# Decode attention with a gated FFN: FFN weights and FFN moved into the K/V loop, projections cut into four column tiles

## The chip, the cores and the metric

The kernel runs on one core of a Trainium2 chip. The metric is device time in microseconds (us) of one execution. A timed execution is a little longer than the span that the profile shows for it (118.14 us for a span of 116.4). The profile is one execution taken by the hardware profiler; "the granted clock" is the share of full speed that the chip gave to the matrix engine (PE). The other engines are DVE (vector), ACT (scalar), POOL and SP; SP issues most of the DMA.

## The reference, cut to what matters

Two rows of 448 numbers go through one decode step. About three quarters of the bytes loaded (32 transfers of 1 MB, out of 44 MB) are the K and V caches of the last 2048 positions.

```python
xn = _layernorm(x)                                  # x: [2, 1, 448]
q = (xn @ wq)                                       # 16 heads of 256, 8 K/V heads
p = softmax(q k^T * 256**-0.5)                      # last W = 2048 of 8192 positions
s = (p v) @ wo                                      # wo: [4096, 448]
g = silu(relu(xn @ w1) @ w2)                        # w1: [448, 1792], w2: [1792, 448]
return x + s * g
```

## The kernel before

One queue (SP) loads everything but the small x, in one order: K0, K1, wq, K2 to K5, V0, V1, then K and V in turn, each transfer 1 MB, and behind the last V the FFN weights w1 and w2 (1.6 MB each) and then wo in five pieces (3.7 MB). wo uses the buffer of wq. Every engine works through its own list in program order.

The loop has eight steps for each K/V head pair k. Work of different pairs is interleaved by step: transpositions of K (`do_T`) run ahead, scores and softmax follow, and the products with V (`do_PV`) come two pairs later:

```python
for k in range(NPAIR):
    e = NCH * k                                     # NCH = 8, NPAIR = 8
    at_step(max(e + 5, NCH - 1), 2, lambda k=k: do_S(k, 0))
    at_step(e + 9, 2, lambda k=k: do_S(k, 1))
    # ... the softmax chain of the pair in steps e + 9 to e + 14
    for s in range(0, NCH, 2):
        at_step(e + 2 * NCH + s, 3, lambda k=k, s=s: do_PV(k, s))
        at_step(e + 2 * NCH + s, 3, lambda k=k, s=s: do_PV(k, s + 1))
```

So step 32 has the transposition of K8 and then the first product with V4. The second argument of `at_step` is the order within a step.

Behind the loop stand the FFN, the gate and the output projection; both products are a single row of full-width matmuls:

```python
for f in range(14):                                 # second FFN product
    m_f = pr.op(PE, mm(sbk[0][0:2, 0:D], h_sb[:, 2 * f:2 * f + 2], w2_sb[:, f * D:(f + 1) * D],
                       f == 0, f == 13), deps)
# ... gate on [2, 448]: exp, + 1, reciprocal, times
for j in range(32):                                 # output projection, D = 448
    m_o = pr.op(PE, mm(obk[0][0:B, 0:D], at2[:, 2 * j:2 * j + 2], wqo[:, j * D:(j + 1) * D],
                       j == 0, j == 31), deps)
# ... times g, plus x, one store of [2, 448]
```

## Time and profile before

| what | value |
|---|---|
| median of three runs | 119.11 us (119.05 to 119.46) |
| span of the profiled execution | 116.4 us (that execution took 118.14 us) |
| DMA stream | about 418 GB/s from 14 us until 107 us |
| last K/V tile landed | 92.9 us |
| last piece of wo landed | 109.3 us |
| attention done (last operand of the projection ready) | 99.3 us |

The landing times are read from the trace's semaphore records. A tile counts as landed when the last of its 16 parts has.

Three rows of the page of the kernel before, in 40 equal slices of the span; a digit is a share in tenths:

```profile
PE   0039828777989498868988977898898365969990
PEclk9999976999999999967999996799999975599999
DMA  3998999999999999999999999999999999999200
```

The DMA is at nine tenths until the 37th slice. The PE is busy throughout, and its clock falls in four places. Next, the timeline of the PE of the kernel before. Columns are start, duration, engine, line of the kernel, operation, output<-inputs, sizes, count, and in brackets the idle time before it and what ended that. L240 is the line of a helper through which most matmuls go, so look at the tile names.

```profile
40.58 0.39 PE L240 MATMUL obk<-vbuf,pt 128*4 128x256 bf16 x8 [1.14 <-DMA vbuf<-in_A_v_cache_dram]
50.56 0.59 PE L240 MATMUL obk<-vbuf,pt 128*4 128x256 bf16 x8 [1.15 <-DMA vbuf<-in_A_v_cache_dram]
60.66 0.39 PE L240 MATMUL obk<-vbuf,pt 128*4 128x256 bf16 x8
70.51 0.39 PE L240 MATMUL obk<-vbuf,pt 128*4 128x256 bf16 x8 [1.01 <-DMA vbuf<-in_A_v_cache_dram]
...
88.89 0.39 PE L240 MATMUL obk<-vbuf,pt 128*4 128x256 bf16 x8
...
98.93 4.10 PE L240 MATMUL sbk<-w_sb,xr 128*4 128x448 bf16 x14
104.64 2.81 PE L240 MATMUL sbk<-w_sb,h_sb 128*2 128x448 bf16 x14 [0.37 <-DVE h_sb L454]
107.28 6.22 PE L240 MATMUL obk<-wqo,at 128*2 128x448 bf16 x32
```

The first product with V of a pair starts at 40.58, 50.56, 60.66 and 70.51 us. Three of the four waited about 1 us for their V tile: the DMA sets the pace. From 88.89 us on there are only the products of the last two pairs and the last pair's chain, and from 98.93 the FFN and the projection in series. The end of the kernel before, all engines without weight loads:

```profile
108.46 2.94 DVE L464 RECIPROCAL tmp<-ea 2x448 f32<-2x448 f32 x1
113.53 0.61 DVE L475 TENSOR_TENSOR tmp<-obk,g_sb 2x448 f32<-2x448 f32 x1 [1.49 <-PE obk L240]
114.18 0.61 DVE L477 TENSOR_TENSOR out_sb<-tmp,x_sb 2x448 bf16<-2x448 f32 x1
114.82 0.31 SPq L36 DMA_DIRECT2D out_dram<-out_sb  x1
```

The reciprocal of the gate (2.94 us on only two partitions) is hidden by the projection. Two further vector operations and the store follow it.

### The profile page before, as it was taken

What the parts mean: (1) busy time and instruction counts of PE and PEld (TensorE: products, weight loads), DVE (VectorE), ACT (ScalarE), POOL (GpSimd) and SP (SyncE); (2) the same over time, 40 slices, a digit from 0 to 9 for tenths busy, and PEclk for the clock granted to TensorE, in tenths of its full rate; (3) what the DMA queues carried; (4) which work ended last, traced back from release to release, by engine and by line L of the source; (5) the groups of instructions that cost most, each with busy time, mean ns of one, the idle gap of its engine ahead of it and who ended that gap; (6) DMA issues with size and microseconds to landing.
All of it is one profiled execution on the core that took longest, in us unless ns stands there. A gap on an engine that the chain in (4) does not pass through costs nothing.

```text
span 116.4 us, 2511 instructions
## 1 busy us (share of the span) xinstructions
PE 86.2 (74%) x1108; PEld 52.7 (45%) x1108; DVE 54.5 (47%) x122; ACT 45.3 (39%) x57; POOL 1.5 (1%) x10
## 2 busy tenths in 40 slices
PE   0039828777989498868988977898898365969990
PEld 0039701445666355634655653566564142334430
DVE  2085401473565654626377371737636443140854
ACT  5913810069565338403834832273673200000100
POOL 5000000000000000000000000000000000000000
PEclk9999976999999999967999996799999975599999
DMA  3998999999999999999999999999999999999200
GB/s 68 420 500 384 453 386 428 417 411 425 425 406 422 425 408 420 425 408 425 417 406 428 414 411 428 417 408 428 422 403 428 435 405 416 436 399 373 85 0 1
DMA packets 5907, 44.27 MB, mean 380 GB/s; under 512 B 645, under 2 KB 905, under 8 KB 1289
## 3 DMA queue, kind: packets, MB, share of 16 engines
q1 hardware_dynamic: 5892, 44.11, 91.6%
q8 instruction: 9, 0.15, 0.5%
q14 instruction: 2, 0.01, 0.0%
q10 hardware_dynamic: 4, 0.00, 0.0%
HBM read 44.11 MB, written 0.00 MB: 379 GB/s over the span
## 4 chain that ended last, share of the span: by engine, by line
DMA 41%; PE 37%; DVE 12%; ACT 5%; issue 1%; SPq 1%; ACTq 0%
DMA vbuf<-in_A_v_cache_dram 41%; PE tb L261 13%; PE obk L240 10%; PE sbk L240 10%; PE mbk L240 4%; DVE o_sb L343 2%; DVE mrow L298 2%; DVE kt L269 2%; DVE rm L290 2%; PE mbk L316 1%; ACT L217 1%; ACT L211 1%; DVE xg L220 1%; ACT obk L211 1%; ACT sbk L211 1%
## 5 line engine op out<-in xcount | busy, mean ns | idle before, releaser
L271 ACT ACTIVATE kt<-tb 128x1024 bf16<-128x1024 bf16 x32 | 32.6, 1024 | 44.0 <-PE tb L261 44.0
L261 PE MATMUL tb<-ident,kbuf 128*128 128x128 bf16 x512 | 41.5, 233 | 0.0
L261 PEld LDWEIGHTS tb<-ident,kbuf 128*128 128x128 bf16 x512 | 33.8, 106 | 7.3 <-issue 7.1
L269 DVE COPY kt<-tb 128x1024 bf16<-128x1024 bf16 x32 | 22.1, 690 | 10.4 <-PE tb L261 10.4
L240 PE MATMUL obk<-vbuf,pt 128*4 128x256 bf16 x256 | 13.4, 297 | 3.5 <-DMA vbuf<-in_A_v_cache_dram 3.5
L240 PE MATMUL sbk<-kt,qz 128*4 128x512 bf16 x128 | 10.8, 407 | 0.6 <-DVE qz L381 0.6
L290 DVE TENSOR_REDUCE rm<-sbk 128x1 f32<-128x512 f32 x8 | 5.5, 692 | 11.1 <-PE sbk L240 11.1
L240 PEld LDWEIGHTS obk<-vbuf,pt 128*4 128x4 bf16 x256 | 4.0, 85 | 7.2 <-DMA vbuf<-in_A_v_cache_dram 4.2
L309 ACT ACTIVATE e_sb<-sbk,bias 128x512 bf16<-128x512 f32 x8 | 5.5, 687 | 3.1 <-DVE bias L305 3.1
L343 DVE TENSOR_SCALAR o_sb<-obk,rs 128x512 bf16<-128x512 f32 x8 | 5.9, 734 | 1.6 <-PE obk L240 1.6
L240 PE MATMUL obk<-wqo,at 128*2 128x448 bf16 x32 | 6.2, 352 | 0.0
L461 ACT ACTIVATE ea<-sbk 2x448 f32<-2x448 f32 x1 | 0.5, 533 | 14.3 <-PE sbk L240 14.3
L240 PE MATMUL mbk<-ident,xg 2*128 2x2 bf16 x7 | 0.3, 164 | 7.7 <-DVE xg L220 7.7
L240 PE MATMUL mbk<-one_f,mrow 1*128 1x1 f32 x16 | 3.0, 256 | 3.8 <-DVE mrow L298 3.8
L321 DVE COPY pt<-mbk 128x64 bf16<-128x64 bf16 x8 | 1.5, 192 | 9.1 <-PE mbk L316 9.1
L298 DVE TENSOR_REDUCE mrow<-mbk 1x128 f32<-1x512 f32 x8 | 5.4, 671 | 0.4 <-PE mbk L295 0.4
L240 PE MATMUL mbk<-fold,o_sb 128*128 128x2 bf16 x32 | 2.0, 168 | 4.4 <-DVE o_sb L343 4.4
L240 PE MATMUL obk<-wqo,xr 128*4 128x512 bf16 x28 | 3.1, 620 | 2.7 <-DMA wqo<-in_A_wq_dram 2.7
L240 PEld LDWEIGHTS mbk<-one_f,mrow 1*128 1x128 f32 x16 | 2.3, 182 | 5.2 <-DVE mrow L298 5.2
L316 PE MATMUL mbk<-ident,e_sb 128*128 128x128 bf16 x32 | 3.2, 222 | 1.6 <-ACT e_sb L309 1.6
L240 PEld LDWEIGHTS obk<-wqo,at 128*2 128x2 bf16 x32 | 2.7, 84 | 3.4
L240 PE MATMUL sbk<-w_sb,xr 128*4 128x448 bf16 x14 | 4.1, 465 | 0.0
(59 smaller groups left out, 47.4 us busy)
## 6 DMA issues: line engine op xcount, KB each, us to landing
kbuf<-in_A_k_cache_dram SPq DMA_DIRECT2D x16, 1024.0 KB, 20.2
vbuf<-in_A_v_cache_dram SPq DMA_DIRECT2D x16, 1024.0 KB, 24.2
wqo<-in_A_wq_dram SPq DMA_DIRECT2D x1, 3584.0 KB, 15.0
w_sb<-in_B_w_dram SPq DMA_DIRECT2D x2, 1568.0 KB, 28.8
wqo<-in_A_wo_dram SPq DMA_DIRECT2D x2, 1120.0 KB, 28.5
wqo<-in_A_wo_dram SPq DMA_DIRECT2D x1, 896.0 KB, 27.7
wqo<-in_A_wo_dram SPq DMA_DIRECT2D x2, 224.0 KB, 25.3
x_sb<-in_A_x_dram ACTq DMA_DIRECT2D x1, 1.8 KB
```

What stands on the lines that cost most here:

```text
L211: a_z = [pr.op(ACTE, lambda e, t=t: e.memzero(t[:, :])) for t in (obk[0], sbk[0], sbk[1], obk[1])]
L217: a_sd = pr.op(ACTE, lambda e: e.activation(sd[0:B, 1:2], sd[0:B, 0:1], ACT.Sqrt), [v_ve])
L240: return lambda e: e.matmul(out_ap, lhsT=lhsT, rhs=rhs, start=start, stop=stop, skip_group_check=True, **kw)
L261: o = pr.op(PE, lambda e, n=n, lo=lo: e.matmul(bank[:, n * 128:(n + 1) * 128], lhsT=src[:, lo:lo + 128], rhs=ident[:, :], start=True, stop ...
L269: evac[i] = pr.op(DVE, lambda e: e.tensor_copy(dst[:, :], bank[:, :]), deps)
L271: evac[i] = pr.op(ACTE, lambda e: e.activation(dst[:, :], bank[:, :], ACT.Copy), deps)
L290: st["rm", k] = pr.op(DVE, lambda e: e.tensor_reduce(out=rm[k % 2][:, :], in_=sbk[k % 2][:, :], axis=AX.X, op=ALU.max), [st["S", k], st.ge ...
L298: st["mrow", k] = pr.op(DVE, lambda e: e.tensor_reduce(out=view(mrow[k % 2], 0, [[32, 4], [1, 32]], n=1), in_=view(mbk, 0, [[0, 4], [1, 32 ...
L309: st["exp", k] = pr.op(ACTE, lambda e: e.activation(e_sb[k % 2][:, :], sbk[k % 2][:, :], ACT.Exp, bias=bias[k % 2][:, 0:1], accum_out=ssum ...
L316: o = pr.op(PE, lambda e, j=j: e.matmul(mb16[:, 512 + 128 * j:640 + 128 * j], lhsT=e_sb[k % 2][:, 128 * j:128 * j + 128], rhs=ident[:, :], ...
L321: st["pt", k] = pr.op(DVE, lambda e: e.tensor_copy(view(pt[k % NP], 0, [[16, 4], [4, 4], [1, 4]]), view(mb16, 512, [[128, 4], [32, 4], [1, ...
L343: st["osb", k] = pr.op(DVE, lambda e: e.tensor_scalar(out=o_sb[k % 2][:, :], in0=obk[k % 2][:, :], scalar1=rs[:, k:k + 1], scalar2=None, o ...
```

## The change

Its intent is to empty the tail. The FFN weights are loaded in the middle of the K/V stream, and the FFN runs inside the loop. The second FFN product and the output projection are cut into four column tiles of 112 columns that go to four separate 32-column strips of the PE, so that four matmuls run at once, and gate and last operations work on 112 columns instead of 448 (on all 128 partitions, eight of which hold results), and the store takes those eight. One score bank is given up for a bank of the FFN.

```diff
+        x_c = named("x_c", [128, NCOL], BF)          # NCOL = D // 4 = 112
+        d_xc = [pr.dma(ACTE, view(x_c, 0, [[1, NCOL]], n=4, p0=b, pstep=32), ...) for b in range(B)]
-        sbk = [psum(f"sbk{i}", [128, 512], F32) for i in range(2)]
+        sbk = psum("sbk", [128, 512], F32)
+        fbk = psum("fbk", [128, 512], F32)
+        for n, fn in enumerate((lambda: do_H(0), lambda: do_H(1), do_hT, do_F)):
+            at_step(4 * NCH + 1 + 2 * n, 6, fn)
         for k in range(NPAIR):
+            if k == 2:
+                loads += [(load_w1, 0, 1), (load_w2, 0, 1)]
             ...                                     # K 2k+4, K 2k+5, V 2k, V 2k+1
-        d_w1 = pr.dma(SP, w1_sb[:, :], w1_src)       # behind the loop
-        d_w2 = pr.dma(SP, w2_sb[:, :]..., w2_src)
         ...
-            m_f = pr.op(PE, mm(sbk[0][0:2, 0:D], h_sb[...], w2_sb[:, f * D:(f + 1) * D], ...
+                for i in range(4):
+                    lo = f * D + i * NCOL
+                    o = pr.op(PE, mm(fbk[32 * i:32 * i + B, 0:NCOL], h_sb[...], w2_sb[:, lo:lo + NCOL],
+                                     f == 0, f == 13, tile_position=(0, 32 * i)), deps)
         ...                                         # the projection in the same way, 32 x 4
-        d_o = pr.dma(SP, out[:, 0, :], out_sb[0:B, :], [v_o])
+        d_o = [pr.dma((SP, ACTE)[b], out[b, 0, :].rearrange("(i n) -> i n", i=4), ...) for b in range(B)]
```

More of the change, by code (lines that the diff above doesn't have):

```diff
@@ L109, in bass_recurrent_scan__sliding_block_cached__dense_activation_relu__decode_kernel @@
     WO_PARTS = [10, 10, 8, 2, 2]
+    NCOL = D // 4
     es = contextlib.ExitStack()
@@ L119, in psum, with view @@
             return es.enter_context(nc.psum_tensor(name, shape, dt))
-        def view(t, off, dims, n=128, p0=0):
+        def view(t, off, dims, n=128, p0=0, pstep=1):
             width = t.shape[1]
-            return bass.AP(t, p0 * width + off, [[width, n]] + dims)
+            return bass.AP(t, p0 * width + off, [[width * pstep, n]] + dims)
         ident = named("ident", [128, 128], BF)
@@ L143, in bass_recurrent_scan__sliding_block_cached__dense_activation_relu__decode_kernel @@
         h_sb = named("h_sb", [128, 28], BF)
-        ea = named("ea", [128, D], F32)
-        g_sb = named("g_sb", [128, D], F32)
-        tmp = named("tmp", [128, D], F32)
-        out_sb = named("out_sb", [128, D], BF)
+        x_c = named("x_c", [128, NCOL], BF)
+        ea = named("ea", [128, NCOL], F32)
+        g_sb = named("g_sb", [128, NCOL], F32)
+        tmp = named("tmp", [128, NCOL], F32)
+        out_sb = named("out_sb", [128, NCOL], BF)
         rm = [named(f"rm{i}", [128, 1], F32) for i in range(2)]
@@ L179, in bass_recurrent_scan__sliding_block_cached__dense_activation_relu__decode_kernel @@
         d_x = pr.dma(ACTE, x_sb[0:B, :], A_x[:, 0, :])
+        p_xc = pr.op(POOL, lambda e: e.memset(x_c[:, :], 0.0))
+        d_xc = [pr.dma(ACTE, view(x_c, 0, [[1, NCOL]], n=4, p0=b, pstep=32),
+                       A_x[b, 0, :].rearrange("(i n) -> i n", i=4), [p_xc]) for b in range(B)]
         d_k, d_v = {}, {}
@@ L209, in bass_recurrent_scan__sliding_block_cached__dense_activation_relu__decode_kernel @@
         p_qz = pr.op(POOL, lambda e: e.memset(qz[:, :], 0.0), [p_one])
-        a_z = [pr.op(ACTE, lambda e, t=t: e.memzero(t[:, :])) for t in (obk[0], sbk[0], sbk[1], obk[1])]
+        a_z = [pr.op(ACTE, lambda e, t=t: e.memzero(t[:, :])) for t in (obk[0], sbk, obk[1], fbk)]
         v_bn = pr.op(DVE, lambda e: e.bn_stats(st6[0:B, :], x_sb[0:B, :]), [d_x])
@@ L273, in do_S @@
         def do_S(k, b):
-            bank = sbk[k % 2]
-            deps = [st["q"], a_z[2]] + ([st.get(("exp", k - 2))] if b == 0 else [])
+            bank = sbk
+            deps = [st["q"], a_z[1]] + ([st.get(("exp", k - 1))] if b == 0 else [])
             for dhi in range(2):
@@ L290, in ch_max @@
             st["rm", k] = pr.op(DVE, lambda e: e.tensor_reduce(
-                out=rm[k % 2][:, :], in_=sbk[k % 2][:, :], axis=AX.X, op=ALU.max),
+                out=rm[k % 2][:, :], in_=sbk[:, :], axis=AX.X, op=ALU.max),
                 [st["S", k], st.get(("rmT", k - 2))])
@@ L309, in ch_exp @@
             st["exp", k] = pr.op(ACTE, lambda e: e.activation(
-                e_sb[k % 2][:, :], sbk[k % 2][:, :], ACT.Exp, bias=bias[k % 2][:, 0:1],
+                e_sb[k % 2][:, :], sbk[:, :], ACT.Exp, bias=bias[k % 2][:, 0:1],
                 accum_out=ssum[k % 2][:, 0:1]), [st["bsb", k], st.get(("Pt", k - 2)), st.get(("gs", k - 2))])
@@ L333, in do_PV @@
             bank, src, p = obk[k % 2], vbuf[c % NVB], pt[k % NP]
-            deps = [d_v[c], st["pt", k], a_z[3]] + ([st.get(("osb", k - 2)), st["q"]] if s == 0 else [])
+            deps = [d_v[c], st["pt", k], a_z[2]] + ([st.get(("osb", k - 2)), st["q"]] if s == 0 else [])
             for i in range(4):
@@ L383, in do_q, with do_H, do_hT, do_F @@
                         view(mb16, 256 * r + b, [[2, 2], [32, 4], [128, 2]])), [o, p_qz])
+        def do_H(u):
+            deps = [st["w1"], a_z[3], st.get("h_n")]
+            for s in range(SLOTS):
+                lo = s * FC + u * (FC // 2)
+                o = pr.op(PE, mm(fbk[0:4, 0:FC // 2], xr[:, 4 * s:4 * s + 4], w1_sb[:, lo:lo + FC // 2],
+                                 s == 0, s == SLOTS - 1), deps)
+                deps = []
+            st["h_n"] = pr.op(DVE, lambda e: e.tensor_scalar(
+                out=h_n[0:4, u * (FC // 2):(u + 1) * (FC // 2)], in0=fbk[0:4, 0:FC // 2],
+                scalar1=0.0, scalar2=None, op0=ALU.max), [o])
+        def do_hT():
+            deps = [st["h_n"]]
+            for j in range(7):
+                o = pr.op(PE, mm(fbk[:, 4 * j:4 * j + 4], view(h_n, j, [[7, 128]], n=4), ident[0:4, 0:4], j == 0), deps)
+                deps = []
+            st["hT"] = pr.op(DVE, lambda e: e.tensor_copy(
+                view(h_sb, 0, [[2, 7], [14, 2], [1, 2]]), view(fbk, 0, [[4, 7], [2, 2], [1, 2]])), [o])
+        def do_F():
+            deps = [st["w2"], st["hT"]]
+            for f in range(14):
+                for i in range(4):
+                    lo = f * D + i * NCOL
+                    o = pr.op(PE, mm(fbk[32 * i:32 * i + B, 0:NCOL], h_sb[:, 2 * f:2 * f + 2], w2_sb[:, lo:lo + NCOL],
+                                     f == 0, f == 13, tile_position=(0, 32 * i)), deps)
+                    deps = []
+            a_e = pr.op(ACTE, lambda e: e.activation(ea[:, :], fbk[:, 0:NCOL], ACT.Exp, scale=-1.0), [o])
+            v_d = pr.op(DVE, lambda e: e.tensor_scalar(
+                out=ea[:, :], in0=ea[:, :], scalar1=1.0, scalar2=None, op0=ALU.add), [a_e])
+            v_rc = pr.op(DVE, lambda e: e.reciprocal(tmp[:, :], ea[:, :]), [v_d])
+            st["g"] = pr.op(DVE, lambda e: e.tensor_tensor(
+                out=g_sb[:, :], in0=fbk[:, 0:NCOL], in1=tmp[:, :], op=ALU.mult), [v_rc])
+        def load_w1(_):
+            st["w1"] = pr.dma(SP, w1_sb[:, :], w1_src)
+        def load_w2(_):
+            st["w2"] = pr.dma(SP, w2_sb[:, :].rearrange("p (hf f) -> p hf f", hf=2), w2_src)
         steps = {}
@@ L424, in bass_recurrent_scan__sliding_block_cached__dense_activation_relu__decode_kernel @@
         assert not loads
-        d_w1 = pr.dma(SP, w1_sb[:, :], w1_src)
-        d_w2 = pr.dma(SP, w2_sb[:, :].rearrange("p (hf f) -> p hf f", hf=2), w2_src)
         d_wo = []
@@ L438, in bass_recurrent_scan__sliding_block_cached__dense_activation_relu__decode_kernel @@
             view(at2, 0, [[2, 32], [1, 2]]), view(mbk, 256, [[1, 32], [32, 2]])), [m_at])
-        deps = [d_w1, st["exp", NPAIR - 2], st["exp", NPAIR - 1]]
-        for u in range(2):
-            for s in range(SLOTS):
-                lo = s * FC + u * (FC // 2)
-                m_h = pr.op(PE, mm(sbk[u][0:4, 0:FC // 2], xr[:, 4 * s:4 * s + 4], w1_sb[:, lo:lo + FC // 2],
-                                   s == 0, s == SLOTS - 1), deps)
-                deps = []
-            v_h = pr.op(DVE, lambda e, u=u: e.tensor_scalar(
-                out=h_n[0:4, u * (FC // 2):(u + 1) * (FC // 2)], in0=sbk[u][0:4, 0:FC // 2],
-                scalar1=0.0, scalar2=None, op0=ALU.max), [m_h])
-        deps = [v_h, v_at2]
-        for j in range(7):
-            m_t = pr.op(PE, mm(mbk_ap(4 * j, 4), view(h_n, j, [[7, 128]], n=4), ident[0:4, 0:4], j == 0), deps)
-            deps = []
-        v_ht = pr.op(DVE, lambda e: e.tensor_copy(
-            view(h_sb, 0, [[2, 7], [14, 2], [1, 2]]), view(mbk, 0, [[4, 7], [2, 2], [1, 2]])), [m_t])
-        deps = [d_w2, v_ht]
-        for f in range(14):
-            m_f = pr.op(PE, mm(sbk[0][0:2, 0:D], h_sb[:, 2 * f:2 * f + 2], w2_sb[:, f * D:(f + 1) * D],
-                               f == 0, f == 13), deps)
-            deps = []
-        a_e = pr.op(ACTE, lambda e: e.activation(ea[0:B, :], sbk[0][0:B, 0:D], ACT.Exp, scale=-1.0), [m_f])
-        v_d = pr.op(DVE, lambda e: e.tensor_scalar(
-            out=ea[0:B, :], in0=ea[0:B, :], scalar1=1.0, scalar2=None, op0=ALU.add), [a_e])
-        v_rc = pr.op(DVE, lambda e: e.reciprocal(tmp[0:B, :], ea[0:B, :]), [v_d])
-        v_g = pr.op(DVE, lambda e: e.tensor_tensor(
-            out=g_sb[0:B, :], in0=sbk[0][0:B, 0:D], in1=tmp[0:B, :], op=ALU.mult), [v_rc])
-        deps = [v_at2, st["osb", NPAIR - 2]]
+        deps = [v_at2, st["g"]]
         landed = dict(d_wo)
@@ L471, in bass_recurrent_scan__sliding_block_cached__dense_activation_relu__decode_kernel @@
             deps = deps + [landed.get(j)]
-            m_o = pr.op(PE, mm(obk[0][0:B, 0:D], at2[:, 2 * j:2 * j + 2], wqo[:, j * D:(j + 1) * D],
-                               j == 0, j == 31), deps)
-            deps = []
+            for i in range(4):
+                lo = j * D + i * NCOL
+                m_o = pr.op(PE, mm(fbk[32 * i:32 * i + B, 0:NCOL], at2[:, 2 * j:2 * j + 2], wqo[:, lo:lo + NCOL],
+                                   j == 0, j == 31, tile_position=(0, 32 * i)), deps)
+                deps = []
         v_t = pr.op(DVE, lambda e: e.tensor_tensor(
-            out=tmp[0:B, :], in0=obk[0][0:B, 0:D], in1=g_sb[0:B, :], op=ALU.mult), [m_o, v_g])
+            out=tmp[:, :], in0=fbk[:, 0:NCOL], in1=g_sb[:, :], op=ALU.mult), [m_o, st["g"]])
         v_o = pr.op(DVE, lambda e: e.tensor_tensor(
-            out=out_sb[0:B, :], in0=tmp[0:B, :], in1=x_sb[0:B, :], op=ALU.add), [v_t])
-        d_o = pr.dma(SP, out[:, 0, :], out_sb[0:B, :], [v_o])
-        pr.op(SP, None, [d_o])
+            out=out_sb[:, :], in0=tmp[:, :], in1=x_c[:, :], op=ALU.add), [v_t, *d_xc])
+        d_o = [pr.dma((SP, ACTE)[b], out[b, 0, :].rearrange("(i n) -> i n", i=4),
+                      view(out_sb, 0, [[1, NCOL]], n=4, p0=b, pstep=32), [v_o]) for b in range(B)]
+        pr.op(SP, None, d_o)
         with nc.Block() as block:
```

## The prediction

> **What bounds it now.** To 70.5 us, the DMA stream: the slices show DMA at 9 of 10 until 107 us, about 418 GB/s, and in the timeline the PE comes early to the first PV of each pair and waits for V, released at 40.58, 50.56 and 70.51 us after 1.0 to 1.2 us idle. A K/V pair lands per 10.0 us; the PE needs 8.8 us for eight steps (60.66 to 69.5). From 70.5 to 88.9 the PE paces, then pair 7's softmax chain (to 99.3), then, in the chain of waits, a serial tail: first FFN product 4.05, relu and transposes 1.6, second product 2.81 (to 107.44), output projection 6.07 (32 matmuls of 448 columns), two DVE ops 1.23, store 1.57. The reciprocal (2.94) hides under the projection. The last weights land near 109.3, so bytes alone would allow a gain of 4 us.
>
> **What the change does.**
> 1. Tail: 8.4 us of FFN leave it. The projection becomes 128 matmuls of 112 columns. Four-tile PV matmuls of 256 columns take 40 ns each (0.32 per 8), more than a quarter of their 107 ns of columns: something per instruction limits them. The Trainium skill, "TensorEngine Tiling (Array Packing)", Instruction Overhead, gives each matmul about 60 cycles however few its columns. Estimate: 128 x 40 to 48 ns = 5.1 to 6.1 us, at most 1 saved. Last DVE ops: 0.26 each, 0.7 saved.
> 2. Loop: w1 and w2 (3.8 us each) stand ahead of K8, K9, V4, V5. K8 lands at 53.6 instead of 46.0, V4 at 58.1 instead of 50.5. The PE works in program order; the PV that needs V4 is in step 32, the FFN in steps 33 to 39, behind it. So the PE, there at 49.4, idles some 8 us (one transposition between) where it idled 1.15, and only then does the FFN: it doesn't fill the hole that its own weights made.
> 3. After the hole: from 58.2, PE work of 8.8 + 8.8 + 8.8 + 8.3, FFN 5.6 (14 x 0.19, transposes 0.35, 56 x 45 ns), and 1.4 for half clock. The skill, "TensorE: Matmul & The Clock Gate", Part 1, says an idle window of 3.4 us halves the clock until a busy one; the trace has 0.5-clock stretches of 3.41 us, the one at 50.4 cost 1.4. Sum: 99.9 at the point that was 88.9. V6 to V15 then land ahead of use (V15 at 100.5); only the 1.0 wait and the dip at 70.5 vanish (counted).
> 4. Pair 7's chain 10.4: 110.3. Projection 5.7: 116.0. DVE 0.55, store 1.6: span 118.1, against 116.4.
>
> The single score bank costs nothing: exp ends 0.35 us before the next scores start. The extra small loads delay the start about 1 us, hidden behind wq (16.7).
>
> **Prediction.** 119.11 + 1.75 = 120.9 us, 118.3 to 123.3. Faster by over 2%: 0.06; within 2%: 0.60; slower by over 2%: 0.34.
>
> **What would show it.** Right: two PE gaps of about 4 us between 49 and 58, ended by K and V loads, granted clock 0.5 after; no later V wait; the eight steps with FFN 15 to 16.5 us; attention done at 109 to 112; projection 5 to 6.3; DMA idle before it ends. Wrong: PE idle there under 4 us, or attention done before 107.
>
> **What would make it wrong.** Tiled matmuls at 25 ns (4 us less in all); the FFN filling waits; a half clock lasting longer; a DMA stall as K14 waits for freed buffers.

## The result and the profile after

The changed kernel takes 117.89 us (117.46 to 118.09, four runs) against 119.10 us of the kernel before in the same rounds. The ratio is 0.9887, with a 95% interval of 0.985 to 0.9923: 1.1% faster. Ratios in this document are the mean time of one kernel's fast runs over that of the other's fast runs of the same rounds, so they are not quite the ratio of the medians that are quoted. Executions over 1.5% slower than the fastest of the same kernel are left out of the means.

The PE's row and its clock on the page of the changed kernel:

```profile
PE   0009945967989689503099898988988988567480
PEclk9999999997699999985559999999999999965569
```

There is now a hole in the PE's row from the 17th to the 20th slice, and the clock is at half for three slices there. The DMA's row has hardly changed (not shown). The timeline of the PE of the changed kernel, in the places shown of before (L246 is the helper now, L267 the transpositions):

```profile
52.90 1.03 PE L267 MATMUL tb<-ident,kbuf 128*128 128x128 bf16 x8 [4.25 <-DMA kbuf<-in_A_k_cache_dram]
57.87 0.60 PE L246 MATMUL obk<-vbuf,pt 128*4 128x256 bf16 x8 [3.94 <-DMA vbuf<-in_A_v_cache_dram]
60.17 2.17 PE L246 MATMUL fbk<-w_sb,xr 128*4 128x448 bf16 x7
64.56 1.49 PE L246 MATMUL fbk<-w_sb,xr 128*4 128x448 bf16 x7
68.27 0.53 PE L246 MATMUL fbk<-ident,h_n 4*128 4x4 bf16 x7
71.08 0.86 PE L246 MATMUL fbk<-w_sb,h_sb 128*2 128x112 bf16 x56
72.42 0.39 PE L246 MATMUL obk<-vbuf,pt 128*4 128x256 bf16 x8
...
98.51 0.39 PE L246 MATMUL obk<-vbuf,pt 128*4 128x256 bf16 x8
...
109.51 2.97 PE L246 MATMUL fbk<-wqo,at 128*2 128x112 bf16 x119 [0.32 <-DVE at L485]
112.95 0.31 PE L246 MATMUL fbk<-wqo,at 128*2 128x112 bf16 x9 [0.47 <-issue]
```

The PE waits 4.25 us for K8 and 3.94 us for V4, and only then, from 60.17 us, come the four FFN groups. The point that was 88.89 us (first product with V of the pair 6) is 98.51 us. The projection begins at 109.51 instead of 107.28, but it is over at 113.3 instead of 113.5 us. Inside it, before the last nine matmuls, stands an idle time of 0.47 us ended by "issue", that is by nothing that the profile shows. The end:

```profile
113.29 0.28 DVE L497 TENSOR_TENSOR tmp<-fbk,g_sb 128x112 f32<-128x112 f32 x1 [3.84 <-PE fbk L246]
113.60 0.28 DVE L499 TENSOR_TENSOR out_sb<-tmp,x_c 128x112 bf16<-128x112 f32 x1
113.91 0.64 SPq L36 DMA_DIRECT2D out_dram<-out_sb  x1
113.91 0.56 ACTq L36 DMA_DIRECT2D out_dram<-out_sb  x1
```

The two last vector operations take 0.28 us each instead of 0.61. The store is slower: from the end of the last vector operation to the landing it takes 1.99 us (113.88 to 115.87) instead of 1.18 (114.79 to 115.97).

Piece by piece, predicted and measured (us):

| piece | predicted | measured | read from |
|---|---|---|---|
| PE idle before V4 | about 8 | 8.2 | brackets at 52.90 and 57.87 |
| eight steps with the FFN | 15.8 | 14.55 | 57.87 to 72.42 |
| of it second FFN product | 2.5 | 0.8 | 71.08 to the next start, 71.87 |
| next 24 steps | 25.9 | 26.1 | 72.42 to 98.51 |
| last pair's chain | 10.4 | 11.0 | 98.51 to 109.51 |
| projection | 5.7 | 3.8 | 109.51 to 113.27 |
| last vector operations | 0.55 | 0.6 | 113.29 to 113.88 |
| store and end | 1.6 | 2.4 | 113.88 to 116.3 |
| span | 118.1 | 116.3 | |

The chain is longer by 0.6 us; it ran at half clock from 102.5 us on, and its four small transpositions, for one, took 0.61 us instead of 0.40. The large differences are the two tiled products: together 3.6 us less than predicted.

### The profile page after: what moved, and what is told of

It is laid out like the page before. It is cut to its first block, busy times and chain, and to the rows that moved or that the text cites. A ratio compares the mean times of both kernels' runs of the same rounds, so it can differ in the third digit from the quotient of the medians.

```text
span 116.3 us, 2783 instructions
## 1 busy us (share of the span) xinstructions
PE 80.1 (69%) x1246; PEld 53.3 (46%) x1246; DVE 50.8 (44%) x122; ACT 45.1 (39%) x57; POOL 1.6 (1%) x11
## 4 chain that ended last, share of the span: by engine, by line
DMA 36%; PE 36%; DVE 18%; ACT 4%; issue 2%; SPq 1%
DMA vbuf<-in_A_v_cache_dram 23%; DMA wqo<-in_A_wq_dram 13%; PE tb L267 11%; PE fbk L246 7%; PE obk L246 6%; PE sbk L246 6%; DVE kt L275 5%; PE mbk L246 4%; DVE o_sb L349 3%; DVE rm L296 3%; DVE mrow L304 3%; PE mbk L322 2%; ACT e_sb L315 1%; ACT L315 1%; SPq L36 1%
## 5 line engine op out<-in xcount | busy, mean ns | idle before, releaser
L267 PE MATMUL tb<-ident,kbuf 128*128 128x128 bf16 x512 | 41.9, 235 | 4.2 <-DMA kbuf<-in_A_k_cache_dram 4.2
L267 PEld LDWEIGHTS tb<-ident,kbuf 128*128 128x128 bf16 x512 | 34.2, 107 | 11.2 <-issue 6.6
L246 PE MATMUL obk<-vbuf,pt 128*4 128x256 bf16 x256 | 13.4, 297 | 4.5 <-DMA vbuf<-in_A_v_cache_dram 4.5
L246 PE MATMUL sbk<-kt,qz 128*4 128x512 bf16 x128 | 10.3, 392 | 1.9 <-ACT e_sb L315 1.4
L296 DVE TENSOR_REDUCE rm<-sbk 128x1 f32<-128x512 f32 x8 | 5.5, 691 | 10.4 <-PE sbk L246 10.4
L246 PEld LDWEIGHTS obk<-vbuf,pt 128*4 128x4 bf16 x256 | 4.0, 85 | 8.2 <-DMA vbuf<-in_A_v_cache_dram 4.9
L246 PE MATMUL mbk<-ident,xg 2*128 2x2 bf16 x7 | 0.3, 163 | 8.9 <-DVE xg L226 8.9
L246 PE MATMUL mbk<-one_f,mrow 1*128 1x1 f32 x16 | 3.0, 256 | 3.9 <-DVE mrow L304 3.9
L246 PE MATMUL mbk<-fold,o_sb 128*128 128x2 bf16 x32 | 2.0, 167 | 4.4 <-DVE o_sb L349 4.4
L246 PEld LDWEIGHTS mbk<-one_f,mrow 1*128 1x128 f32 x16 | 2.3, 182 | 5.4 <-DVE mrow L304 5.4
L246 PEld LDWEIGHTS mbk<-ident,xg 2*128 2x128 bf16 x7 | 0.3, 101 | 8.9 <-DVE xg L226 8.9
L246 PEld LDWEIGHTS mbk<-fold,o_sb 128*128 128x128 bf16 x32 | 1.4, 99 | 6.0 <-DVE o_sb L349 6.0
L322 PEld LDWEIGHTS mbk<-ident,e_sb 128*128 128x128 bf16 x32 | 2.0, 106 | 4.0 <-issue 3.0
L246 PE MATMUL fbk<-wqo,at 128*2 128x112 bf16 x128 | 3.3, 292 | 0.8 <-issue 0.5
L246 PE MATMUL fbk<-w_sb,xr 128*4 128x448 bf16 x14 | 3.7, 409 | 0.0
```

The lines of the kernel that those rows point to most:

```text
L246: return lambda e: e.matmul(out_ap, lhsT=lhsT, rhs=rhs, start=start, stop=stop, skip_group_check=True, **kw)
L267: o = pr.op(PE, lambda e, n=n, lo=lo: e.matmul(bank[:, n * 128:(n + 1) * 128], lhsT=src[:, lo:lo + 128], rhs=ident[:, :], start=True, stop ...
L296: st["rm", k] = pr.op(DVE, lambda e: e.tensor_reduce(out=rm[k % 2][:, :], in_=sbk[:, :], axis=AX.X, op=ALU.max), [st["S", k], st.get(("rmT ...
L322: o = pr.op(PE, lambda e, j=j: e.matmul(mb16[:, 512 + 128 * j:640 + 128 * j], lhsT=e_sb[k % 2][:, 128 * j:128 * j + 128], rhs=ident[:, :], ...
```

## The experiments

Theory A: the column tiles make the gain and moving the FFN costs, since the PE works in program order and leaves the hole empty that the weights make in the stream. Theory B keeps the prediction's price of a tiled matmul: the tiles bring at most 1 us, so whatever is gained comes from moving. (The prediction itself expected moving to cost.) A third theory, C, came up after the first four runs. All results were correct. The summary first; "before" had a median of 119.3 to 119.5 us in these rounds, and of 119.10 in those of the changed kernel. The ranges include slow runs: one of halves, two of tile_align, one of tile_lean.

| run | what it is | median us (range) | ratio to before (95%) |
|---|---|---|---|
| changed kernel | | 117.89 (117.46 to 118.09) | 0.9887 (0.985 to 0.9923) |
| tile_only | tiles, FFN behind the loop | 115.56 (115.44 to 115.84) | 0.969 (0.9622 to 0.9758) |
| move_only | FFN in the loop, no tiles | 128.28 (128.1 to 129.87) | 1.079 (1.0685 to 1.0895) |
| fill | both, FFN ahead of step 32 | 115.9 (115.64 to 116.42) | 0.9727 (0.9662 to 0.9793) |
| halves | both, 56 columns per matmul | 124.47 (123.92 to 125.86) | 1.0426 (1.0345 to 1.0507) |
| after_align | both, 120 PE instructions more | 117.74 (117.41 to 118.05) | 0.9885 (0.9842 to 0.9929) |
| store_sp | both, stores from one queue | 118.64 (118.04 to 118.88) | 0.9956 (0.9913 to 1.0) |
| fill_align | fill, 120 PE instructions more | 115.42 (115.29 to 115.7) | 0.9697 (0.965 to 0.9745) |
| tile_align | tile_only, 120 more | 116.9 (115.3 to 117.36) | 0.9738 (0.9656 to 0.982) |
| fill_lean | fill, 32 PE instructions fewer | 114.31 (114.03 to 115.13) | 0.9563 (0.9502 to 0.9624) |
| tile_lean | tile_only, 32 fewer | 114.75 (113.89 to 115.73) | 0.9562 (0.9492 to 0.9633) |

### The two halves of the change: tile_only and move_only

tile_only takes the FFN and its weights back behind the loop and keeps the tiles:

```diff
-            at_step(4 * NCH + 1 + 2 * n, 6, fn)      # FFN in the loop
-            if k == 2:
-                loads += [(load_w1, 0, 1), (load_w2, 0, 1)]
+        load_w1(0); load_w2(0)                       # behind the loop
+        do_H(0); do_H(1); do_hT(); do_F()            # banks sbk and fbk; gate reads sbk
```

> Undoes one half: the FFN and its weights are back behind the loop, as before; column tiles, gate and store stay as in the changed kernel. Theory A (the tiles make the gain and moving the FFN costs): the end is set by the DMA stream, last weights at 109.3 us, then the last two j of the projection 0.3, two DVE ops 0.6, store 2.4: span about 112.6, ratio to before about 0.968; second FFN product about 0.9 to 1.5 us instead of 2.81. Theory B (moving the FFN makes the gain, the tiles bring at most 1 us as predicted): about 1 to 2 us faster than before, ratio 0.985 to 0.99.

move_only keeps loads and FFN in the loop, but puts back 448-column matmuls, the gate and the last operations on two rows, and the old store:

```diff
-                for i in range(4): ... mm(fbk[32 * i:32 * i + B, 0:NCOL], ..., tile_position=(0, 32 * i))
+                o = pr.op(PE, mm(fbk[0:2, 0:D], h_sb[:, 2 * f:2 * f + 2], w2_sb[:, f * D:(f + 1) * D], ...
```

> The other half alone: weights and FFN in the loop, but 448-column matmuls without column tiles, gate, last ops and store on two rows as before. Theory A: hole of about 8 us on the PE as in the changed kernel, FFN 2 us longer in the loop, projection about 6.1 again, last ops 1.23: span 119 to 122.5, ratio 1.03 to 1.05, slower than before. Theory B: faster than before, ratio about 0.99.

The tiles alone gave 3.1%, moving alone cost 7.9%, and both together gain 1.1%. Theory A stands, theory B falls. The span of tile_only was 114.0 us and not 112.6, because the last weights landed at 110.52 us and not at 109.3; why is taken up below. The tail of tile_only, PE:

```profile
104.51 0.86 PE L246 MATMUL sbk<-w_sb,h_sb 128*2 128x112 bf16 x56 [0.37 <-DVE h_sb L408]
105.19 1.16 PE L246 MATMUL fbk<-wqo,at 128*2 128x112 bf16 x80
107.80 0.82 PE L246 MATMUL fbk<-wqo,at 128*2 128x112 bf16 x39 [1.45 <-DMA wqo<-in_A_wo_dram]
110.68 0.44 PE L246 MATMUL fbk<-wqo,at 128*2 128x112 bf16 x9 [2.06 <-issue]
```

The second FFN product takes 0.7 us (to 105.19) instead of 2.81, and the first 80 matmuls of the projection take 1.2 us. Then the PE waits for pieces of wo. The stream of weights, not the PE's speed, sets this end. That was the room that the prediction saw ("bytes alone would allow a gain of 4 us") and gave away through its price for a tiled matmul.

move_only was worse than expected by either theory (span 128.1 against 119 to 122.5):

```profile
80.15 0.36 PE L298 MATMUL mbk<-ident_f,rm 128*1 128x128 f32 x1 [3.02 <-DVE rm L293]
116.90 8.30 PE L243 MATMUL fbk<-wqo,at 128*2 128x448 bf16 x32 [0.32 <-DVE at L480]
```

In the loop the gate on two partitions of 448 columns occupies the DVE when the loop needs it for evacuations and maxima; the PE waits 3.02 us for a maximum. The granted clock is half from 80.2 to 87.0 us and again from 110.9 to 121.2, so that the projection takes 8.30 us where it took 6.22. Of the 11.8 us over the changed kernel, 7.4 lie before the projection begins (116.90 against 109.51) and 4.5 in it; the 7.4 were not split further. So the tiles are also what makes the gate cheap enough for the loop: 0.85 us for its reciprocal on 112 columns against 2.94.

### The hole: fill

The four FFN groups are put ahead of the transposition of step 32. By then w1 and w2 have landed or nearly so, and K8 has not:

```diff
-            at_step(4 * NCH + 1 + 2 * n, 6, fn)
+            at_step(4 * NCH, -1, fn)
```

> The changed kernel with the four FFN steps put ahead of the transposition of step 32, so in the hole before K8 lands, instead of in steps 33 to 39. Theory A (in-order PE leaves its hole empty): PE idle between 48 and 58 us falls from 8.2 to about 4 us, the eight steps after V4 take 8.8 to 9.5 instead of 14.5 us, the PE waits again for V6 or V8 (67.8, 77.7), attention is done near 107, then the last weights (108.8) set the end: span about 112.2, ratio to before about 0.965. Rival (the place of the FFN in the loop doesn't matter, since the stream and pair 7's chain decide): same as the changed kernel, 0.989.

```profile
48.67 1.49 PE L246 MATMUL fbk<-w_sb,xr 128*4 128x448 bf16 x7
53.95 0.86 PE L246 MATMUL fbk<-w_sb,h_sb 128*2 128x112 bf16 x56 [0.37 <-DVE h_sb L407]
57.89 0.60 PE L246 MATMUL obk<-vbuf,pt 128*4 128x256 bf16 x8 [2.52 <-DMA vbuf<-in_A_v_cache_dram]
77.81 0.39 PE L246 MATMUL obk<-vbuf,pt 128*4 128x256 bf16 x8 [0.56 <-DMA vbuf<-in_A_v_cache_dram]
87.75 0.39 PE L246 MATMUL obk<-vbuf,pt 128*4 128x256 bf16 x8 [1.09 <-DMA vbuf<-in_A_v_cache_dram]
...
106.90 2.96 PE L246 MATMUL fbk<-wqo,at 128*2 128x112 bf16 x119 [0.32 <-DVE at L485]
110.82 0.44 PE L246 MATMUL fbk<-wqo,at 128*2 128x112 bf16 x9 [0.96 <-issue]
```

The FFN runs from 48.67 to 54.8 us in the hole. The PE waits for V8 and V10 again (0.56 and 1.09 us), so it has caught up with the stream. Ratio 0.9727 against 0.9887 for the changed kernel: the place of the FFN cost 1.6%. The expected ratio of 0.965 was missed by about 1 us and the expected span of 112.2 by 2.1 us, and the gap before the last nine matmuls is there again, 0.96 us long.

### The price of a tiled matmul: halves

Each tiled matmul of 112 columns becomes two of 56: twice the instructions, the same columns.

```diff
+                for hc in range(2):
                   for i in range(4):
-                    mm(fbk[32 * i:32 * i + B, 0:NCOL], ..., w2_sb[:, lo:lo + NCOL], f == 0, ...)
+                    mm(fbk[32 * i:32 * i + B, c0:c0 + NCOL // 2], ..., w2_sb[:, lo:lo + NCOL // 2], f == 0 and hc == 0, ...)
```

> The changed kernel with every tiled FFN and projection matmul of 112 columns split into two of 56: twice the instructions, the same columns. If columns limit (four tiles at a time): second FFN product stays near 0.82 us, projection near 3.3 us at the half clock, time as the changed kernel. If something per instruction limits, as the prediction said: the product takes about 1.6 us or more and the projection 5 us or more, time 2 to 3 us longer.

```profile
71.26 1.06 PE L246 MATMUL fbk<-w_sb,h_sb 128*2 128x56 bf16 x112
73.12 0.45 PE L267 MATMUL tb<-ident,kbuf 128*128 128x128 bf16 x5
77.08 0.50 PE L267 MATMUL tb<-ident,kbuf 128*128 128x128 bf16 x3 [3.51 <-issue]
...
114.37 2.41 PE L246 MATMUL fbk<-wqo,at 128*2 128x56 bf16 x191 [0.32 <-DVE at L488]
118.15 0.95 PE L246 MATMUL fbk<-wqo,at 128*2 128x56 bf16 x65 [1.37 <-issue]
```

The product of 112 matmuls runs from 71.26 to 72.25 us (start of what follows), 8.8 ns each. In the changed kernel 56 matmuls ran from 71.08 to 71.87, 14.1 ns each. Doubling the instructions at the same columns adds a quarter, not twice the time. In the projection at half clock, 119 matmuls of 112 columns took 22.4 ns each (109.51 to the end of the start times at 112.18), and 191 of 56 columns 11.4 ns each (114.37 to 116.55): half the time for half the columns. So columns set the pace at 112 columns, and the prediction's 40 to 48 ns per instruction was wrong by a factor of two to three. The "per instruction" of the product with V was a fixed part of each group: its 8 matmuls of 256 columns are two sets of four, whose starts are 109 ns apart (40.575 and 40.684 us), so columns account for 2 x 109 ns = 0.22 us of the 0.32. Spread over eight matmuls, the other 0.10 us looks like 13 ns each; it isn't paid again with each further matmul.

The start times in the traces show where the fixed part stands. In the changed kernel sets of four start together, 47 ns from set to set at full clock: 11.8 ns per matmul, no more than the columns (112/256 x 109 / 4 = 11.9). The transposition behind the last matmul of the second FFN product starts 145 ns after it. In tile_only, where another tiled product follows, the next matmul starts 38 ns after it. So about 0.11 us is paid where a transposition follows a tiled group, once per group. What it consists of no run here separates. The transposition's own weight load (98 ns in the kernel before) is one candidate. The Trainium skill, "TensorEngine Tiling (Array Packing)", section Key Properties, says that a change of tiling mode drains the engine, which would fit as well. In halves at full clock the starts are 7.9 ns apart on average, where 56 columns on four tiles would be 6.0: at that size some 2 ns per instruction show as well.

Nevertheless halves was 4.3% slower than before. Its PE stands still for 3.51 us in the middle of a transposition group, between the fifth and the sixth matmul, and for 1.37 us in the projection, both ended by "issue".

### Where the gaps stand: instruction blocks

I listed the PE's records (weight loads, matmuls and the few semaphore instructions) in order of start and counted to each gap. In halves the long gap stands before record 1474 and the other before 2753; in the changed kernel and in tile_only the gap stands before 2497, in fill before 2498. Up to one record these are 1474, 1474 + 4 x 256 and 1474 + 5 x 256. The Trainium skill, "Runtime: NRT & Kernel Launch", section Instruction fetch mechanics, says that instructions come in blocks of 256, 16 KiB each, by a DMA queue of the sequencer's own, and that crossing a border is "mostly hidden". The trace has that queue. The line of the DMA view, kernel before, then halves (packets, MB, share of 16 DMA engines):

```profile
q8 instruction: 9, 0.15, 0.5%
```

```profile
q8 instruction: 11, 0.18, 0.6%
```

Each packet has 16384 bytes and took 0.9 to 1.4 us. Times from the packet and instruction records (us):

| run | border | block before it entered | packet on the queue | PE goes on | PE idle at the border (ended by "issue") |
|---|---|---|---|---|---|
| halves | 1474 | 71.28 | 74.60 to 75.70 | 77.08 | 3.51 |
| changed | 2498 | 107.06 | 110.06 to 111.47 | 112.95 | 0.47 |
| fill | 2498 | 104.44 | 108.30 to 109.33 | 110.82 | 0.96 |
| tile_only | 2498 | 105.05 | 108.38 to 109.49 | 110.68 | 2.06 |
| halves, stream over | 2754 | 115.06 | 115.78 to 116.76 | 118.15 | 1.37 |

In the four waits where the block before was entered while the stream ran, the block could be used 5.6 to 6.4 us after that; with the DMA idle, 3.1 us. The stream is not the whole of the difference: over all runs the packet starts 0.3 to 3.9 us after the block before is entered, and in the changed kernel it starts 1.3 us after the last weights have landed (108.78). In tile_only the last weights landed at 110.52 us, just before the PE went on, so there the two waits end together. The loop takes about 10 us for a block and never waits. 128 pairs of weight load and small matmul, which fill a block, take 1.8 to 2.9 us at 14.1 to 22.4 ns. Theory C: a run of about a block of small matmuls, or more, outruns its own instructions.

after_align adds 60 idle matmuls at the very start, where the PE has nothing to do, and so shifts the border from matmul 119 of the projection to matmul 59, with the block before it entered early in the last chain:

```diff
+        for _ in range(60):
+            pr.op(PE, mm(mbk_ap(300, 2, 2), ident[:, 0:2], ident[:, 0:2], True, True), [p_id])
```

> The changed kernel with 60 matmuls of two columns on constants added at the very start, where the PE is idle before 8.9 us; they compute nothing that is used. Theory C: the gaps of the PE inside the projection (0.47 us in the changed kernel, 0.96 with the filled hole, 1.37 and 3.5 with 56 columns) stand at instructions 1474, 2498 and 2753 of the PE's list, multiples of 256 apart, and are waits for the next block of 256 instructions (16384 bytes on the instruction queue), which comes 5.5 to 6.4 us after the block before it is entered while the weights stream, longer than dense small matmuls take for 256. 120 more instructions ahead move the border inside the projection from matmul 119 to 59 and its block is asked for at about 100 us: the gap is gone, span 0.4 to 0.5 us shorter, ratio to before about 0.985. Rival (the gap belongs to the last weight landings or to the clock's change at 112.7): the gap stays before the same matmul, time as the changed kernel.

fill_align and tile_align are the same addition to fill and tile_only.

> FFN in the hole and 120 more PE instructions at the start. Theory C: the 0.96 us gap near the end of the projection is gone, projection ends at about 110.1 instead of 111.3, span about 113.2, ratio to before about 0.963 (0.973 without). Rival: gap and time stay as with the FFN in the hole alone.

> Column tiles only, FFN behind the loop, and 120 more PE instructions at the start. Theory C: the border moves to matmul 59 of the projection, the 2.06 us gap before the last nine matmuls shrinks to the wait for the last weights, which land at 109.3 instead of 110.5 because no instruction block of 1.1 us stands ahead of their last packet: span about 112.8, ratio to before about 0.959. Rival (the last weights land late for another reason): landing near 110.5 and span 114.0 again.

The projection of after_align, in one piece; then that of fill_align:

```profile
110.02 3.16 PE L246 MATMUL fbk<-wqo,at 128*2 128x112 bf16 x128 [0.32 <-DVE at L488]
```

```profile
106.64 2.04 PE L246 MATMUL fbk<-wqo,at 128*2 128x112 bf16 x80 [0.32 <-DVE at L488]
109.25 1.50 PE L246 MATMUL fbk<-wqo,at 128*2 128x112 bf16 x48 [0.58 <-DMA wqo<-in_A_wo_dram]
```

The gap ended by "issue" is gone in all three. The times moved little: 0.9885 after 0.9887, 0.9697 after 0.9727, and for tile_align two of its four runs were slow, the other two 115.3 and 116.58. In after_align the projection began 0.51 us later (110.02 against 109.51), which used up what the gap had cost; why is not shown. Part of the expectation failed: the last weights did not land early. In fill_align they landed at 110.35 us against 109.0 in fill, in tile_align at 110.16 us, where 109.3 was expected, against 110.52 in tile_only. The landing records show why. A DMA counts as landed when its 16 parts have landed, one part per DMA engine (the Trainium skill, "DMA: Bandwidth & Descriptors", section "Why a DMA increments its semaphore by 16 and not by 1"). Landing times of the first, 8th, 14th, 15th and last part of the last piece of wo:

| run | first | 8th | 14th | 15th | last |
|---|---|---|---|---|---|
| fill | 107.04 | 108.06 | 108.73 | 108.83 | 109.00 |
| fill_align | 107.02 | 108.13 | 108.77 | 108.84 | 110.35 |
| tile_only | 107.17 | 108.32 | 108.80 | 108.88 | 110.52 |

In fill one part of each tile lands 1.4 us after the others from 22.95 us on, right after the first block of 20.3 to 21.3 us, and it stays late; more parts join it as more blocks come. I read this as one of the 16 DMA engines held up by each block and staying behind. As long as each block meets a DMA engine that is not yet late, the last part lands no later. In fill only eight blocks come before 108 us; in fill_align a ninth comes from 99.97 to 101.08 us, and from the next piece on one part is late a second time (104.33 us against 102.81 of the part before it). So 120 idle instructions bought one gap and paid one more block in the stream. (The expectation of fill_lean below calls it the tenth; that is wrong by one.)

fill_lean tests this the other way round, with fewer instructions. Two small products of each softmax chain go from float32 to bfloat16, so each is one weight load and one matmul instead of two, 32 PE instructions in all:

```diff
-        one_f = named("one_f", [128, 1], F32)
+        one_f = named("one_f", [128, 1], BF)        # likewise mrow, ssum, gsum
```

> FFN in the hole, and the two small float32 products of each softmax chain (bias column and row sum) in bfloat16: each takes one weight load and one matmul instead of two, so the PE's list is 32 instructions shorter (the small loss of precision is meant; result must still be correct). Theory C (blocks of 256 instructions): the border that stood before matmul 119 of the projection falls behind its end, the border before it lands at matmul 7 and is entered after 106.9 us, so its block is fetched after the weight stream: no gap in the projection and no late weights, unlike the run with 120 instructions more, where the gap went but a tenth block came into the stream and the last weights landed at 110.4. Last weights near 109.0, projection ends near 110.1, span about 113.0, ratio to before about 0.96. Rival (gap and late weights have other causes): gap of about 1 us stays, span 114.0 or more.

> Column tiles only, FFN behind the loop, with the same two products in bfloat16. Theory C: no border before the last nine matmuls any more, but the border at matmul 7 is entered near 105.3 us, before the stream ends, and its block is fetched near 108.5, so the last weights may still land late (110.5). Span 113.5 to 114.0 if they do, 112.8 if they land at 109.3; ratio 0.959 to 0.968.

```profile
106.17 3.23 PE L246 MATMUL fbk<-wqo,at 128*2 128x112 bf16 x128 [0.32 <-DVE at L487]
```

```profile
107.91 1.08 PE L246 MATMUL fbk<-wqo,at 128*2 128x112 bf16 x40 [1.52 <-DMA wqo<-in_A_wo_dram]
110.35 0.36 PE L246 MATMUL fbk<-wqo,at 128*2 128x112 bf16 x8 [1.36 <-DMA wqo<-in_A_wo_dram]
```

In fill_lean the 128 matmuls run in one piece, the last weights land at 109.01 us and the span is 112.3 us. But the expectation was wrong on one point: the block was not fetched after the stream. It came from 108.10 to 109.21 us, about when it came in fill and in tile_only. The packet records show what differs. In fill_lean and in fill the last piece of data was moved at 108.52 and 108.38 us, before the block's end, so nothing was left for it to delay. In tile_only one packet of 4 bytes, in tile_lean four data packets follow the end of the block, and the last part lands late. The projection also starts 0.73 us earlier than in fill; the change of precision and the shift of the border are not separated by this run. In tile_lean no border stands before the last matmuls, but a block comes at 108.03 us, and the last weights land at 110.31, as expected for that case; its PE waits for the DMA, not for instructions. Its six times fall into two groups: 113.9 to 114.1 at a mean granted clock of 0.944 to 0.945, and 115.4 to 115.7 at 0.90 to 0.916. Only one of the upper was traced. Whether the lower group is the one with weights in time, or the clock makes the groups, stays open.

Both lean versions beat the two kernels: 0.956 to the kernel before. fill_lean has the lowest median, 114.31 us.

### The store: store_sp

```diff
-        d_o = [pr.dma((SP, ACTE)[b], out[b, 0, :]...
+        d_o = [pr.dma(SP, out[b, 0, :]...
```

> The changed kernel with both stores issued from one queue (SP) one after the other instead of SP and ACT at once. From the end of the last DVE op to the landing took 1.18 us before and 1.99 us in the changed kernel. If the two queues disturb each other: 0.2 to 0.4 us shorter. If the four short pieces of 224 bytes cost it: the same or 0.3 us longer, since the second issue waits for the first.

```profile
114.04 1.19 SPq L36 DMA_DIRECT2D out_dram<-out_sb  x2
```

Two stores of four pieces of 224 bytes take 1.19 us to issue from one queue, 0.6 each, where the one store of two pieces of 896 bytes took 0.31. The last landed 2.26 us after the last vector operation (114.01 to 116.27), against 1.99 with two queues and 1.18 before. One queue is slower, but the two queues do disturb each other. With two, the SP store landed 1.96 us after its issue began (113.91 to 115.87) and the ACT store 1.61 us (to 115.52); as the first of two on one queue, the SP store took 1.63 us (114.04 to 115.67). The disturbance of 0.3 us costs less than the second issue. Against the 1.15 us of the old store (114.82 to 115.97), the short pieces cost about 0.5 us. The run was 0.7% slower than after_align (0.9956 against 0.9885), which also has the 120 more instructions.

## Why the prediction was wrong

The prediction was 120.9 us, 118.3 to 123.3. The measurement, 117.89 us, lies below the range, and the kernel became faster where it was predicted to become slower. That it still fell within 2%, the likeliest outcome by the prediction (0.60), is partly luck: the 3.6 us that it overestimated were in part made up by what it underestimated. Most of its mechanism held:

- "The PE, there at 49.4, idles some 8 us": measured 4.25 + 3.94 us, ended by K8 and V4 as said, at half clock from 51.3 to 61.5 us. fill showed that the hole is only so expensive because the FFN stands behind it.
- "V6 to V15 then land ahead of use": no later wait for V in the changed kernel.
- "DMA idle before it ends": the last weights landed at 108.8 us, before the projection began.
- "The single score bank costs nothing": the steady loop shows no wait for it, only one of 1.36 us in the first pair, at 26.94 us, which is early enough to be absorbed.

The step that failed is the first: "something per instruction limits them ... 128 x 40 to 48 ns = 5.1 to 6.1 us, at most 1 saved", and with it "56 x 45 ns" in the FFN. Measured were 14.1 ns per matmul at full clock and 22.4 at half clock, 0.8 us for the second FFN product and 3.8 us for the projection with its gap: 3.6 us less than the sum had. The rate was taken from groups of eight, where a fixed part of 0.10 us is a third of the time. A group of 32 was in the same profile (1.88 us at half clock, 59 ns each where the columns alone are 53) and would have told. The prediction even named the case ("Tiled matmuls at 25 ns") among what would make it wrong.

Three smaller steps went the other way: the store was taken as before (1.6 us, measured 2.4), the last pair's chain was 0.6 us longer, and nothing was allowed for instruction supply (0.47 us, within the 3.8 above).

A last part is a matter of the base. The difference of 1.75 us between spans was put on the median of 119.11 us, but the profiled execution of before was a quick one, 118.14 us. The two profiled spans differ by only 0.1 us, the two medians by 1.2 us. On the 118.14 us of the profiled execution, the same difference would have given 119.9. Later the fast executions of the kernel before had spans of 116.6 to 118.9 us, so what the others spend more lies inside the span; where is not shown by any run.

## What to carry to other kernels

An engine that works in program order doesn't use a hole in its input by itself: if weights are put into a stream ahead of data, put the work that needs the weights ahead of the work that needs the delayed data (1.6% here), and test the parts of a change alone, since here one part alone gained 3.1%, and with the other 1.1% was left. Take the rate of a small instruction from the longest run of it in the profile, never from a short group with a fixed part. Where many small matmuls are packed together, count them: 256 weight loads and matmuls are one block of instructions, which must come through DMA engines that the data uses too, and an idle time ended by "issue" at a fixed distance of 256 is the sign.

## What the Trainium skill lacked or had wrong

- "Runtime: NRT & Kernel Launch", Instruction fetch mechanics, has the blocks of 256 instructions right, but calls their cost mostly hidden; it gives the PE room for 2048 instructions and in a note two blocks in all, and only the note fits. Here the PE waited 0.47 to 3.51 us at such borders, and a block was fetched only after the one before it was entered: usable 5.6 to 6.4 us later when that one was entered under a full data stream, 3.1 us later without.
- None of the pages used here says in so many words that an instruction block delays data: each took 0.9 to 1.4 us, and behind the first one in fill one part of each later tile landed about 1.4 us late; with one part late twice (fill_align), the last weights landed at 110.35 instead of 109.0 us.
- "TensorE: Matmul & The Clock Gate", Part 1, says that starts of matmuls are never closer than about 25 ns, and "TensorEngine Tiling (Array Packing)", Instruction Overhead, says about 60 cycles each. With four column tiles the starts at full clock were 11.8 ns apart on average at 112 columns and 7.9 ns at 56 (14.1 and 8.8 ns with the pause behind the group).
- "DMA: Bandwidth & Descriptors" treats short pieces as a matter of bandwidth. Here the issue grew too: 0.56 to 0.64 us for four pieces of 224 bytes, 0.31 us for two of 896, some 0.3 us of the 0.5 that the short pieces cost.
